# A windowed-attention and gated feed-forward kernel: the same 2127 works issued in another order

## The chip, the cores and the metric

One core of a Trainium2 chip. The metric is the device time of one execution in microseconds (us). Half a per cent of it, 2.6 us, is about the least that a measurement of this kernel can tell from nothing. The engines are PE (matrix products), DVE, ACT and POOL (elementwise work), and SP, which here only issues transfers. Each has its own queue and works through it strictly in order.

## The reference

Attention over 8 batches, 8 heads, 576 tokens and 64 dimensions per head, where each token sees itself and the 63 before it; its output, as rows of 512 numbers, goes through a gated feed-forward block with a convolution over three tokens:

```python
scores = scale * np.matmul(q, k.transpose(0, 1, 3, 2))
mask = (rel >= 0) & (rel < window)
scores = np.where(mask, scores, -1000000000.0)
scores = scores - np.max(scores, axis=-1, keepdims=True)
attn = np.exp(scores)
attn = attn / (np.sum(attn, axis=-1, keepdims=True) + 1e-09)
x = np.matmul(attn, v)
...
h = np.maximum(x @ w_in, 0.0)          # 512 -> 1024
for k in range(K):                     # K = 3 taps over the tokens
    conv_out += conv_w[k][None, None, :] * hp[:, k:k + S, :]
gate = 1.0 / (1.0 + np.exp(-conv_out))
return (h * gate @ w_out)              # 1024 -> 512
```

All inputs to the products are 32-bit; the three weights arrive as 64-bit words and are decoded on the chip.

## The kernel before, in words

The 4608 tokens are cut into 12 units of 384 tokens (six blocks of 64). For each unit the attention makes x, four chunks c of 128 features by 384 tokens; then eight blocks f of 128 hidden features follow, worked in pairs.

One unit, as a chain of works: `load_*` (SP) bring queries, keys and values. `scores` (PE) fill banks of PSUM. `row_max` (DVE) adds a mask and takes the row's maximum, so it waits for scores and mask. `exps` (ACT) takes exponentials with their sums; `guard` (DVE or POOL) adds 1e-9, `reciprocal` (DVE), `normalise` (DVE or POOL). In units 0 and 1 (64-row blocks) PE turns the result (`turn`, `unturn` copies it out); later units use DVE's `transpose` and `place` transfers. `values` (PE) multiplies by v into a bank, and `split_hi` (a rounded copy, xh) and `split_lo` (the rest, xl, always DVE) write x as two parts.

Then per block f: `mm1` (PE, 12 matmuls: each of four chunks with w_hi.xh, w_lo.xh, w_hi.xl), `relu` (ACT or DVE, empties the bank into `hbuf`), `conv_mid` and two `conv_side` (the three taps), and per pair `sigmoid` (ACT), `gate` (DVE or POOL), `gate_hi` and `gate_lo` (the two parts gh, gl), and `mm2` (PE, three matmuls each). `result` copies the sums out and `store` writes them. Units 0 to 2 do f 0 to 3 first, in turn, and f 4 to 7 later (`TASKS`), since the weights are still arriving and being decoded.

Decoding a weight block: `load_w` (SP), `magnitude` (ACT or DVE), `shift`, `sign` (DVE), `low` (ACT), `add_low` (DVE), `larger` (any of three: the rounded part) and `lo` (DVE or POOL: the rest). Two buffers `wx` pass from one block to the next.

Three masks are made by POOL (`make_mask`): mask 0 for units 0 and 1 (`first_masks`), mask 1 for all other blocks and mask 2 for blocks at a sequence's start (`later_masks`; the first such 32-row block comes in unit 3). `fill` issues matmuls on a spare tile, whose results nobody uses.

The order of all this is no scheduler's: `plan()` numbers the 2127 works, and the table `ORDER` lists these numbers in the order of issue. A letter behind a number (A, D, P) sets the engine (ACT, DVE, POOL) of a work that has a choice; `/k` sets its PSUM bank; `Fn/k` is n fill matmuls into bank k. Works on one engine keep the table's order; between engines semaphores on the data and on the buffers decide.

Of the kernel before, what the change touches and what calls it, by code (L numbers as in the profile page):

```python
# [120 lines left out]
def plan():  # L121
# [121 lines left out]
    41 7 13 3 80 9 5 6 86 4 8 0 81 F5/0 40/2 97 1 59/4 42 22/6 43 60 198 31/2 82 83 23 32 195 44 194 24 87D F3/0  # L243
    12/4 45D 46 88 25 89 50/6 33 14 193 26P 47P 196 34 27 197 51 28P F2/1 48/0 11 15 10 35D 16 36 29/1 37D 139
    84 98D 62 38/4 17D 18 99 61 19P 30D 220/2 39D 52 63P 95 20/5 85 211 64 53 221 65P 210/6 21A 54D 49A 55 F1/1
    201/2 212 56P 101 229/4 66/1 222 202 154 57/0 506 67A 100 248/6 58A 238/2 102 90 74/1 249 214 103P 315 138
    104P 77/0 230 213 118 71/7 75A 91 239 231 68/6 215P 78D 92P 204 216 76 93P 72D 69A 79 141A 217P 70 203 73
    316 223 F5/4 94/1 117 140D 142 199 251 224D 225 148 232 226P 240 218/4 144 143 120A 227/5 205P 105/0 242 145
    228D 317 146P 250 440 206 2 207D 168 96A 119A 233D 147D 208/6 241 321/2 234 121 209A 122 153/7 219A 127 107A
    252P 323 243P 235P 123 106D 149 318 260/1 253 124 326 200 257/0 254P 244 322 261A 155A 262 319 327 245P 258D  # L250
    324 150 343 F3/6 246/5 110A 108 236/6 325 109 255/4 111 332/2 247A 328P 256A 125D 151P 329 237A 333 637 152P
    128 439 334 169 335 F3/1 263/7 112 336 357/2 330P 259 338 264D 266/1 265 337 359 126P 156/0 113 320 331 638
    339P 340 341D 267A 114P 342 157A 161A 268 350 363 358 F3/5 269/7 353 368 129 354 158D 351 170D 130A 356 346
    272/0 270 361 162 347 131D 360 345 163 349 362 159 643/2 639 160 115A 352 290/1 364D 365 366D 171A 355 271A
    344 116P 367 174 348 164 645 293/7 369 371 172 173 376 274A 175 133/5 370 165D 378 134/6 176A 273A 379 132/4
    178 166A 640 136 291 377 179 177D 135 277A 373 275 137 442A 167D 374 384/0 292A 380 276 294A 375 381/1 295A
    644 445 372 183 278 441A 279 184 385A 443 654/2 280 180 185 382A 386 801 181P 649 655 390/7 182P 383 387/0
    656 455 188 281P 298A 642 388D 391A 641 186 389 660 469 392 678/2 521 659 449 490 187 470 299 282A 491 393/1
    300 802 191A 283D 450 647 296 657 396/0 444 297 658 679 301 661P 446 286/6 451 414/7 447P 680 394 662 302P
    189D 395A 190A 417/1 475 192 398A 452D 471A 415 663D 397A 285/5 303A 399 288 496 304D 284/4 418A 401A 289  # L260
    400 416A 287 402 472A 403 305 448D 308 404 453D 306 803 419A 493D 520 307 405D 492A 646 310 420 454/0 494
    495 501 497 500 309 498A 473 422A 457/1 499D 311A 313A 502 648 406D 505/7 407D 684 456A 650P 423 480 503D
    681 408/4 504D 474 683 410/6 476 508/0 312A 479 458A 314 682 651 421 804 481 459A 409/5 462A 424 413 509A
    460 425 545/1 461 685D 677 652D 531 411 426P 686 653 507A 412 664 548/0 668 463 427A 464 672 477A 428D 666
# [36 lines left out]
    1464 1236 1467 1483D 1123 1127A 1268/7 1251D 1126D 1255A 1504 1256 1220/4 1237 1257 1622 1357/0 1128 1465
    1462 1360/1 1497 1222/6 1358A 1238P 1361A 1221/5 1469 1362 1223 1359 1225 1505P 1391 1506 1254 1271/1 1239A
# [542 lines left out]
```

## Time and profile before

| | |
|---|---|
| median of three runs | 519.61 us (517.9 to 519.64) |
| profiled execution | 519.21 us, of it the span 517.4 us |
| mean granted clock of PE | 0.997 |
| PE busy | 503.0 us, 97% of the span |
| DVE, ACT, POOL busy | 399.6, 335.4, 167.2 us |

A time in a row of the profile counts from the start of the span. A timeline row has start, duration, engine, line, operation, output and inputs, count, and in brackets how long the engine had been idle before and what ended that. A row of the groups has the busy sum, the mean duration in ns, and the idle time before. Lines are those of the kernel before.

### The profile page before, as it was taken

What the parts mean: (1) busy time and instruction counts of PE and PEld (TensorE: products, weight loads), DVE (VectorE), ACT (ScalarE), POOL (GpSimd) and SP (SyncE); (2) the same over time, 40 slices, a digit from 0 to 9 for tenths busy, and PEclk for the clock granted to TensorE, in tenths of its full rate; (3) what the DMA queues carried; (4) which work ended last, traced back from release to release, by engine and by line L of the source; (5) the groups of instructions that cost most, each with busy time, mean ns of one, the idle gap of its engine ahead of it and who ended that gap; (6) DMA issues with size and microseconds to landing.
All of it is one profiled execution on the core that took longest, in us unless ns stands there. A gap on an engine that the chain in (4) does not pass through costs nothing.

```text
span 517.4 us, 13998 instructions
## 1 busy us (share of the span) xinstructions
PE 503.0 (97%) x5377; PEld 441.3 (85%) x5377; DVE 399.6 (77%) x1197; ACT 335.4 (65%) x922; POOL 167.2 (32%) x261
## 2 busy tenths in 40 slices
PE   8888979999999999999999999999999999999997
PEld 5677859988898898888888899889889889989996
DVE  5989989898968697887687768778585657675881
ACT  5999788986875865883782784792388386332420
POOL 5678233033340400340332241061335332212311
PEclk9999989999999999999999999999999999999999
DMA  8987339332544452364554165355234411400022
GB/s 300 359 352 245 114 110 346 148 112 70 194 101 141 85 186 78 101 165 126 179 181 139 29 197 169 110 177 174 58 106 154 150 64 63 148 6 2 1 99 84
DMA packets 27714, 72.76 MB, mean 141 GB/s; under 512 B 5760, under 2 KB 14080, under 8 KB 27648
## 3 DMA queue, kind: packets, MB, share of 16 engines
q1 hardware_dynamic: 27216, 69.52, 40.8%
q0 software_dynamic: 432, 2.36, 2.6%
q8 instruction: 42, 0.69, 0.5%
q14 instruction: 24, 0.20, 0.1%
HBM read 48.26 MB, written 11.80 MB: 116 GB/s over the span
## 4 chain that ended last, share of the span: by engine, by line
PE 86%; DVE 10%; POOL 2%; issue 1%; ACT 1%; POOLq 0%; DVEq 0%
PE bank L718 36%; PE bank L639 36%; PE bank L622 6%; PE bank L536 5%; PE bank L723 3%; DVE s L557 3%; DVE c L688 1%; DVE wx L453 1%; POOL mask L491 1%; DVE xl L632 1%; DVE s L583 1%; DVE T L602 1%; DVE wx L446 1%; DVE sm L572 1%; POOL mask L493 0%
## 5 line engine op out<-in xcount | busy, mean ns | idle before, releaser
L639 PE MATMUL bank<-xh,w_in 128*128 128x384 f32 x768 | 196.6, 336 | 0.3 <-DVE xl L632 0.2
L718 PE MATMUL bank<-w_out,gh 128*128 128x512 f32 x528 | 169.6, 402 | 0.0
L639 PEld LDWEIGHTS bank<-xh,w_in 128*128 128x128 f32 x768 | 139.4, 188 | 7.1 <-ACT hbuf L665 0.4
L639 PE MATMUL bank<-xl,w_in 128*128 128x384 f32 x384 | 129.1, 336 | 0.7 <-DVE xl L632 0.7
L688 DVE SCALAR_TENSOR_TENSOR c<-hbuf,cw,c 128x386 f32<-128x386 f32 (+1 forms) x192 | 122.8, 661 | 8.8 <-ACT c L681 7.3
L718 PEld LDWEIGHTS bank<-w_out,gh 128*128 128x128 f32 x528 | 96.1, 188 | 19.4 <-issue 0.3
L567 ACT ACTIVATE s<-s,nm 128x96 f32<-128x96 f32 (+2 forms) x288 | 105.2, 368 | 9.2 <-DVE nm L557 8.9
L718 PE MATMUL bank<-w_out,gl 128*128 128x512 f32 x264 | 104.6, 396 | 0.0
L699 POOL TENSOR_TENSOR c<-c,hbuf 128x386 f32<-128x386 f32 (+5 forms) x44 | 50.8, 1171 | 145.2 <-ACT c L692 145.2
L665 ACT ACTIVATE hbuf<-bank 128x384 f32<-128x384 f32 x70 | 33.4, 486 | 67.0 <-PE bank L639 64.9
L639 PEld LDWEIGHTS bank<-xl,w_in 128*128 128x128 f32 x384 | 72.1, 188 | 1.1 <-DVE xl L632 1.0
L557 DVE CUSTOM_DVE_ANT_0 s<-bank,mask 128x96 f32<-128x96 f32 (+2 forms) x288 | 56.4, 254 | 18.2 <-PE bank L536 12.2
L692 ACT ACTIVATE c<-c 128x772 f32<-128x772 f32 (+1 forms) x48 | 40.7, 849 | 30.7 <-DVE c L688 30.4
L718 PEld LDWEIGHTS bank<-w_out,gl 128*128 128x128 f32 x264 | 49.7, 188 | 11.8
L567 ACT ACTIVATION_READ_ACCUMULATOR s<-s,nm 128x1 f32 x288 | 54.4, 189 | 0.0
L583 POOL TENSOR_TENSOR s<-s,r 128x768 f32<-128x768 f32 (+1 forms) x24 | 33.9, 1414 | 49.3 <-DVE r L576 49.1
L681 ACT ACTIVATE c<-hbuf,cw 128x386 f32<-128x386 f32 (+1 forms) x59 | 35.6, 613 | 17.5 <-DVE hbuf L667 8.9
L622 PEld LDWEIGHTS bank<-ub,v 128*64 128x64 f32 x1152 | 35.7, 138 | 9.4 <-issue 3.6
L536 PEld LDWEIGHTS bank<-qk 64*32 64x32 f32 (+1 forms) x2112 | 30.7, 113 | 14.0 <-issue 7.2
L622 PE MATMUL bank<-ub,v 128*64 128x64 f32 x1152 | 38.7, 224 | 3.2 <-ACT hbuf L665 2.8
L536 PE MATMUL bank<-qk 64*32 64x96 f32 (+2 forms) x2112 | 40.5, 260 | 1.3 <-DMA qk<-in_first_dram 0.7
L709 DVE TENSOR_TENSOR gl<-c,gh 128x768 fp32r<-128x768 f32 (+1 forms) x33 | 32.8, 995 | 6.4 <-ACT gh L704 6.0
(79 smaller groups left out, 538.1 us busy)
## 6 DMA issues: line engine op xcount, KB each, us to landing
v<-in_v_dram SPq DMA_DIRECT2D x24, 768.0 KB, 5.6
ub<-T SPq DMA_DIRECT2D x240, 48.0 KB, 2.0
qk<-in_k_dram SPq DMA_DIRECT2D x20, 448.0 KB, 5.0
out_dram<-ot SPq DMA_DIRECT2D x11, 768.0 KB, 4.5
qk<-in_q_dram SPq DMA_DIRECT2D x20, 384.0 KB, 4.2
raw_in<-in_w_in_dram SPq DMA_DIRECT2D x8, 512.0 KB, 8.3
raw_out<-in_w_out_dram SPq DMA_DIRECT2D x8, 512.0 KB, 8.8
qk<-in_first_dram SPq DMA_DIRECT2D x12, 320.0 KB, 4.9
```

The source lines that it names most:

```text
L536: nc.tensor.matmul(banks[bank[h]][r:r + rows, i * P + o:i * P + k], qq[hs, s:s + rows], kk[hs, s + o:s + k], start=True, stop=True)
L557: nc.vector.tensor_tensor_reduce(out=ss[n // NB][:, n % NB, h, o:k], in0=banks[bank[h]][:, i * P + o:i * P + k], in1=mask[m][:, o:k], scal ...
L567: nc.scalar.activation(x, x, AF.Exp, bias=small(nms, (n,))[:, h:h + 1], scale=-1.0, accum_out=small(sms, (n,))[:, h:h + 1])
L583: engine[on].tensor_tensor(sv, sv, small(rs, ns).unsqueeze(2).broadcast_to([P, 2 * len(ns), k]), ALU.mult)
L622: nc.tensor.matmul(banks[bank[0]][h * D:(h + 1) * D, t * W:(t + 1) * W], vs[:, c, t, h], ub[g][:, 2 * p:2 * p + 2, 2 * t + h], start=True, ...
L639: nc.tensor.matmul(banks[bank[0]][:, :NX], w[:, a, c], y[x][:, c], start=(c == 0 and j == 0), stop=(c == NC - 1 and j == 2))
L665: nc.scalar.activation(out, ps, AF.Relu)
L681: nc.scalar.activation(c, h, AF.Copy, scale=w)
L688: nc.vector.scalar_tensor_tensor(c, h, w, c, op0=ALU.mult, op1=ALU.add)
L692: nc.scalar.activation(both(u, j), both(u, j), AF.Sigmoid)
L699: engine[on].tensor_tensor(c[:, :, a:a + n], c[:, :, a + o:a + o + n], h[:, :, 1 + a + o:1 + a + o + n], ALU.mult)
L718: nc.tensor.matmul(banks[bank[0]], x, wts["out", f][:, w], start=(start and i == 0), stop=(stop and i == 2))
```

## The change

Only the table `ORDER` is another; every one of its 100 lines differs, so a line of it tells nothing. The same 2127 works are issued; the fill matmuls are 22 where they were 25.

```
-    41 7 13 3 80 9 5 6 86 4 8 0 81 F5/0 40/2 97 1 59/4 42 22/6 43 60 198 31/2 82 83 23 32 195 44 194 24 87D F3/0
...
```

Engines, of the works that have a choice (before, after): gate 27 on POOL and 21 on DVE, now 21 and 27; relu 70 on ACT and 26 on DVE, now 63 and 33; conv_mid 59 on ACT and 37 on DVE, now 55 and 41; split_hi 24 and 24, now 29 on ACT and 19 on DVE; normalise 24 on POOL and 18 on DVE, now 22 and 20; magnitude 11 on ACT and 5 on DVE, now 9 and 7; larger 6 on ACT, 4 on DVE, 6 on POOL, now 8, 2, 6; lo 6 on POOL and 10 on DVE, now 9 and 7; gate_lo keeps 33 on DVE and 15 on POOL, but not the same ones. `gate_lo` of the very first pair goes from POOL to DVE.

POOL at the program's start, before. Names end in a serial number; mask0, mask1 and mask2 are the three masks, s0 to s2 the score tiles, ident the identity for the turns.

```order
L493 AFFINE_SELECT mask2_77<-mask2_77 32x96
L496 MEMSET mask2_77 32x32
L487 MEMSET mask0_75 128x128
L491 AFFINE_SELECT mask0_75<-mask0_75 64x128
L493 AFFINE_SELECT mask0_75<-mask0_75 64x128
```

After, from the first instruction of the kernel's own on:

```order
L549 MEMSET s0_81 128x2x64
masks.py:197 MEMSET ident_78 128x128
masks.py:199 ISA
masks.py:199 AFFINE_SELECT ident_78<-ident_78 128x128
L648 MEMSET hbuf_69 128x2x2
L649 MEMSET hbuf_69 128x2
L654 MEMSET hbuf_69 128x2
L549 MEMSET s1_82 128x2x64
```

Eight rows of mask 2's selects stood ahead of mask 0 and now come much later; ahead of mask 0 there are now the identity, the blanks and memsets of `hbuf`. Mask 1 follows right behind mask 0, and mask 2 is made here, in the middle of the normalisations of units 0 and 1:

```order
L473 TENSOR_TENSOR w_in0_474<-wx0_70,w_in0_474 128x512
L583 TENSOR_TENSOR s0_81<-s0_81,r0_90 128x512 x2
L487 MEMSET mask2_77 128x128
L491 AFFINE_SELECT mask2_77<-mask2_77 32x96
L493 AFFINE_SELECT mask2_77<-mask2_77 32x96
L496 MEMSET mask2_77 32x64
```

So POOL carries mask 2 at a time when DVE has decoding and splitting to do.

SP at the program's start, before. raw_in0 and raw_in1 are the first two blocks of w_in, cbits the convolution's weights, and `first` the packed queries and keys of units 0 and 1, burst by burst.

```order
L407 DMA qk_79<-in_first_dram 128x640
L428 DMA cbits_74<-in_conv_w_dram 128x48
L407 DMA qk_79<-in_first_dram 128x640 x3
L424 DMA raw_in0_151<-in_w_in_dram 128x1024
L407 DMA qk_79<-in_first_dram 128x640 x2
L424 DMA raw_in1_182<-in_w_in_dram 128x1024
L407 DMA qk_79<-in_first_dram 128x640 x6
```

After:

```order
L407 DMA qk_79<-in_first_dram 128x640
L424 DMA raw_in1_121<-in_w_in_dram 128x1024
L407 DMA qk_79<-in_first_dram 128x640 x5
L424 DMA raw_in0_176<-in_w_in_dram 128x1024
L407 DMA qk_79<-in_first_dram 128x640 x6
```

The block raw_in1 comes right behind the first burst, ahead of the other eleven; raw_in0 stands behind six bursts where it stood behind four; the convolution's weights come later.

ACT around the relus of unit 1 in its first turn, before. w_out2 is the rounded part of a weight block, raw_* the words that `low` works on.

```order
L692 ACTIVATE c1_94<-c1_94 128x772
L681 ACTIVATE c0_93<-hbuf_69,cw_73 128x386
L469 CAST w_out2_1071<-wx0_70 128x512
L665 ACTIVATE hbuf_69<-bank0_104 128x2x192
L704 CAST gh1_96<-c1_94 128x2x384
L449 ACTIVATE raw_out3_812<-raw_out3_812 128x512
L681 ACTIVATE c0_93<-hbuf_69,cw_73 128x386
L436 ACTIVATE wx1_71<-raw_in5_586 128x512
L665 ACTIVATE hbuf_69<-bank1_105 128x2x192
```

After:

```order
L692 ACTIVATE c1_94<-c1_94 128x772
L449 ACTIVATE raw_out3_711<-raw_out3_711 128x512
L665 ACTIVATE hbuf_69<-bank0_104 128x2x192
L449 ACTIVATE raw_in4_930<-raw_in4_930 128x512
L449 ACTIVATE raw_out2_720<-raw_out2_720 128x512
L704 CAST gh1_96<-c1_94 128x2x384
L665 ACTIVATE hbuf_69<-bank1_105 128x2x192
L469 CAST w_out2_1084<-wx0_70 128x512
```

The cast of w_out2, which stood ahead of the relus, stands behind them.

More of the change, by code (lines that the diff above doesn't have):

```diff
@@ L248 @@
[L248 to L252, printed above, removed]
@@ new lines @@
+    96A 227/4 85 251 143 317 218/5 145 199 246/7 106A 107A 208/6 252D 146D 147D 151A 321/2 120A 119D 153/0 152P
+    209A 322 110A 253 123 121 232 108 156/1 127 228A 318 155A 233P 219D 200 254P 128 169 234 323 325 168 235P
+    260/0 157D 326 129 255/6 327 122 236/4 256A 109 261A 124 324 F2/5 332/2 111 247A 125P 257/1 237A 328P 333
+    637 130P 161A 491 263/7 131P 334 258A 319 336 329 264D 343 338 265 330D F3/5 266/7 337 357/2 112 335 162
+    267A 259 339P 126P 113 262 638 340 268 320 341P 359 F3/5 269/1 439 171A 331 170A 114P 342 363 358 272/0 350
@@ new lines @@
+    506 508/1 684 677 668 479 683 666 459D 672 460 507A 685P 409/5 674 474 509A 513A 676 412 461 435A 476 670
+    818/2 480 686 514 667 545/7 477A 687D 675 510A 671 437A 478P 688 465 314 820 430 699 548/0 481 669 515 673
+    526 466D 482A 694 690 819 566/1 546 698 547A 511 467A 689 512 483D 693 516 569/7 468D 642 522A 696 523D 821
+    524 665 842/2 517D 691 433 700 525 695 567 843 486/6 714 436A 697 527 484/4 568A 692 550D 485/5 528A 549D
+    518A 487 844 553A 488 551 848 529D 489 519D 822 701/1 570A 554 710/0 574A 530 707/7 846 552 535 711A 532
@@ new lines @@
+    702A 555 536 823 533P 703 807/2 556 575 534P 591/1 808 965 824 557D 537 809 592 540 593D 845 538 571D 558D
+    847 539 712 559P 594/1 543A 541D 966 542A 813 825D 572 704/0 826 595A 827P 812 560/4 805 705A 438 562/6 810
+    706 561/5 576 599A 612/1 573 708A 811 849D 600 601 577 850 709 615/0 851D 841 578P 852 564 713/7 862 613
+    579A 735 859 616A 854 580D 614A 565 857 596D 583 597 856 814D 716/0 861 598 815 967 816D 602 864 620A 817
+    582 617A 828 563 603D 835 581 832 584 621 863 618 586 839 619 734/1 589A 622 840 587A 855 604A 968 715A 585
@@ new lines @@
+    1131 753 869A 1015P 766 870 751 754 781D 731 991D 749 767P 867 779/0 1132 978D 590 979 980D 970 877/7 780A
+    782 768A 1005 784A 981 880/1 769D 783 771 785 881A 752 786 879A 992 774 787 1016 898/0 788P 1023 1027 1146/2
+    1024 900D 941 789A 1018 885D 901/1 1022 790D 1019 886 1025 1148 792 995 902A 1147 770 903A 996 906A 772 994
+    904 1152 773 882D 999 887 1021 791 907 997 1170/2 908 1028 905 775 969 883 909 998 793 1171 1017 796 884
+    1002 919/7 1172 1020 888 910D 1026 1175 1000 889P 795 993 922/0 1003 920 890D 921A 1004 911D 940/1 1176 1001
@@ new lines @@
+    891P 923A 1149 794 942A 1063 1135/2 1173 1042 912P 1150 1038/7 1293 799A 1032/0 1039D 1174 636 1035/1 1040
+    797A 924D 1029/7 798A 1136 1151 892/4 1033D 1030A 1137 894/6 1153P 1177P 1036A 927A 895 1031 1139 1178 1294
+    897 928 1138 1154 893/5 929 925 915 1141 1034 918 1140 926 896 1179D 930 943/7 1142P 1037 945A 914 931D 944A
+    1041/0 1295 1155D 932A 1169 948A 933P 1180 917 1044/1 1143 1181 949 1191 1144P 1192 935 1296 1045A 1183 913
+    1049A 946 1190 1062/7 1084 1145 947 950 916 1050 951 938 1156 1043A 1051 936 1157 1064A 1046D 1310/2 1134
@@ new lines @@
+    1047 1185 1048 1065/1 1184 1311 1182 952D 1186 1083/0 1158 953D 1166 954D 1133 1312 1067A 956 1066D 1316
+    1334/2 1189 1070D 1068 1161 959 1071 1165 1335 939 1315 1160 957 1336 1187 1085A 934 1052 1188 1069 937 1072
+    1299/2 1073 955 1053D 1457 1314 1162 1086/7 1074D 1164 1075D 1168 1054D 1167 1340 1202/1 1301 1055P 1159
+    1199/0 962D 1203A 1087A 960 1204 1313 1200D 1458 958 963A 1300 1163 1317P 1104/7 1091A 800 1318 1319D 1304
+    1298 1338 1201 1076D 1058/6 1339 1057/5 1337 1061 1088A 1459 1341P 1193/1 1105 1303 1206 1106D 1196/0 1092
@@ new lines @@
+    1194A 1305 1060 961D 1197A 1093 1079 1302 1198 1078 1195 1082 1089 1107/7 1109D 1306D 1110 1307 1333 1308P
+    1056/4 1460 1108D 1205/0 1111 1112A 1090 1309 1094 1208/1 1342 1113 1343D 1095P 1344 1059 1209A 1226/7 1346
+    1297 1114 1347 1227 1320 1115 1348 1081 1096D 1327 1207D 1474/2 1097P 1353 1229/1 1321 1476 1326 1475 1116P
+    1479 1352 1100 1247/0 1325 1210D 1248 1322 1211 1351 1117D 1230D 1349 1498/2 1249A 1118D 1350 1213A 1077
+    1477 1332 1214 1250/1 1356 1478 1212 1345 1499 1330 1215 1080 1331 1228D 1216 1355 1103 1234D 1235 1354 1121
@@ new lines @@
+    1251D 1329 1099 1500 1480 1323 1102 1236 1124 1217D 1098 1502 1120 1370 1503 1123 1363/0 1501 1126D 1366/7
+    1218A 1231D 1232 1101 1504 1233 1463/2 1364A 1367D 1505P 1481P 1237 1269 1482 1219P 1268/1 1368 1621 1465
+    1328 1324 1252A 1119 1270D 1127A 1221/5 1255D 1365 1271/7 1238D 1256 1239A 1622 1464 1122 964 1272A 1253
+    1222/6 1125A 1257 1360/1 1254 1357/0 1483D 1361A 1258 1220/4 1506 1362 1358A 1223 1259P 1469 1623 1359 1225
+    1461 1369/7 1240P 1468 1467 1372/1 1507P 1273A 1466 1624 1243 1276A 1470D 1471 1260D 1371A 1224 1472P 1497
@@ new lines @@
+    1241 1508 1244 1274 1242 1517 1391 1373D 1128 1245 1473 1390/0 1484 1261D 1489 1487 1638/2 1277 1377A 1513
+    1278 1374A 1246 1496 1275 1264 1639 1512 1279 1267 1515 1640 1262 1518 1375 1491 1662/2 1644 1490 1393/7
+    1663 1493 1494 1280D 1642 1509 1664 1263 1488 1433 1412 1495 1265 1281D 1667 1378 1511 1627/2 1668 1379 1519
+    1411/1 1641 1282D 1486 1516 1643 1394D 1785 1398D 1520 1645P 1392D 1283 1376 1485 1266 1646 1395D 1514 1380
+    1285 1396 1492 1399 1284 1462 1628 1286 1510 1400 1414/7 1381P 1629 1786 1288 1415A 1397 1287 1382A 1413D
@@ new lines @@
+    1432/0 1401 1383D 1632 1402P 1530/7 1524/1 1434A 1531D 1534 1291A 1555 1527/0 1532 1647P 1631 1289D 1521/7
+    1626 1528A 1787 1386/6 1290A 1403D 1522A 1389 1404D 1630 1385/5 1665 1523 1384/4 1529 1525A 1388 1419D 1633
+    1661 1435/7 1416A 1420 1437A 1526 1666 1417 1533/0 1669D 1436D 1670 1671D 1440A 1788 1625 1418 1292 1407
+    1438 1387 1421 1406 1441 1422 1409 1442 1634D 1405 1635 1672 1636P 1536/1 1423D 1410 1424D 1554/7 1576 1637
+    1648 1439 1660 1802/2 1425D 1556A 1682 1443 1408 1679 1803 1537A 1655 1557/7 1541A 1444D 1659 1805 1656
@@ new lines @@
+    1445D 1649 1804 1426 1658 1558D 1428 1680 1446D 1826/2 1653 1575/1 1654 1828 1675 1535D 1650 1832 1538D 1652
+    1559D 1806 1431 1539 1657 1808 1429 1827 1684 1427 1562D 1673 1829 1542 1447 1677 1540 1807 1578/7 1676 1543
+    1678 1809P 1560 1544 1651 1561 1683 1449 1810 1563 1681 1430 1564 1579A 1674 1450 1545D 1565 1452 1546D 1830
+    1791/2 1698 1577D 1547P 1688/0 1793 1949 1455A 1691/7 1792 1797 1566P 1694/1 1689D 1453A 1692D 1448 1794
+    1550/6 1795 1811D 1451 1567A 1597 1693 1553 1695D 1831 1950 1596/7 1583D 1584 1796 1696 1580A 1798P 1833D
@@ new lines @@
+    1585 1685/1 1690 1825 1548/4 1834 1799 1686D 1551 1800P 1454D 1599/0 1687 1456 1568D 1789 1951 1581 1549/5
+    1600A 1835D 1552 1598A 1601A 1569 1801 1570 1582 1571 1602 1586 1697/1 1812 1836 1843 1604A 1700/0 1587D
+    1790 1844 1588A 1740 1719 1573 1589D 1701A 1574 1603 1952 1718/7 1817 1705D 1605 1841 1706 1823 1606 1818
+    1591 1607 1822 1594 1848 1699A 1721/0 1702A 1821 1720A 1847 1703 1704 1838 1966/2 1707 1820 1722D 1592 1816
+    1708 1967 1837 1739/1 1968 1839 1970 1846 1608D 1842 1572 1845 1609A 1590 1819 1741A 1990/2 1610P 1824 1971
@@ new lines @@
+    1814 1742/7 1992 1840 1815 1709D 1726A 1813 1969 1595 1723D 1991 1996 1760/0 1724 1994 1710D 1993 1727
+    1955/2 1728 1995 1725 1593 1743A 1997P 1761 1729 1613 1762D 1612 1711D 1858/1 1747D 1972 1748 1849/7 1730D
+    1855/0 1616 1749 1954 1859A 1973P 1957 1611 1856D 1615 1961 1860 1614 1619A 1956 1852/1 1960 1744D 1857
+    1714/6 1617A 1974 1618A 1745 1717 1853A 1731D 1958 1713/5 1850D 1732P 1716 1998 1959 1851 1763/0 1854 1746
+    1975P 1861/7 1764A 1750 1999P 1989 1864/1 1765A 1862 1883 1768A 1962P 1751P 1963 2000 1734 1882/0 2006 1964D
@@ new lines @@
+    1752A 2002 2012 1904 1766 1735 1620 1965 2003 1738 2011 1712/4 1863D 2001 1769 1715 2009 1865D 1733 1753D
+    1953 1736 1770 1737 1866D 1756 1976 1767 1759 1988 1885/7 1771 1984 1985 1884A 1772D 2005 2010 1903/1 1773D
+    2007 1774D 1986 1886D 1983 1869D 1755 1887D 1981 1870 1754 1982 1867 1906/0 1978 1868 1987 1871 2008 1888
+    1872 1757 1979 1890A 1777 2004 1873P 1977 1758 1980 1780 1925 1776 1874A 1779 1905A 1875P 2022/7 1782A 1907A
+    2019/1 2023D 1783A 2016/0 2024 1891 2013/7 2017A 1911D 1775 2020D 1892 1778 1889 1878/6 2021 1781A 1877/5
@@ new lines @@
+    2018 1893 1784 1881 1908A 1894P 1876/4 1924/1 1895A 1927/0 1896D 2014D 1912 1880 2015 1928A 1909 1899 1926A
+    1932A 1929D 1898 1930 1902 1913 2025/7 1910 1933 1914 1931 1915D 2028/0 1916D 1934 1917P 1879 1935 2048/1
+    2026 2049 2027D 2029A 1936P 1901 2033A 1897 1919 2030D 1920 2072 1937D 1923 2095 2031 1900 2032 2051/0 1938D
+    2050D 2034 1941 2052A 1944 2056D 2035 1922 2057 1918 2036 2071/7 2053A 2037P 2074/1 2054 2038A 2058 2055
+    2073D 1921 2039D 1940 2075D 1943 2076D 2079A 1939 2059 2094/0 2080 1947A 2060D 2077 2061A 2043/7 2081 1942
@@ L343 @@
+    1946A 2078 2097/1 2062D 2082 2083P 2041/5 2098D 2045 2096D 2102A 2042/6 2099D 2047 1945D 2046 2084D 1948
+    2040/4 2085D 2044 2064 2100 2068 2103 2087 2101 2066 2104 2063 2091 2105 2067 2065 2106P 2086 2069 2090
+    2107D 2070 2108D 2089 2093 2088 2109 2112 2092 2116 2113 2125 2123 2110 2117D 2114 2118 2111 2119D 2124 2115
+    2126 2120 2121A 2122
 """
```

115 lines of the change are left out of this document (21 added, 94 removed).

## The prediction

> **What bounds the kernel now.** I read the page's busy shares first, then the waits of PE, then windows over the front, then the timelines of DVE, ACT and POOL at the places where PE waits.
>
> ```profile
> span 517.4 us, 13998 instructions
> PE 503.0 (97%) x5377; PEld 441.3 (85%) x5377; DVE 399.6 (77%) x1197; ACT 335.4 (65%) x922; POOL 167.2 (32%) x261
> ```
>
> PE is the bound: of 517.4 us it is idle for only 14.4. Where PE waits, in full (us in total, times, longest):
>
> ```profile
> PE bank L590 <- POOL s L583: 3.2, 4, 1.1
> PE bank L622 <- ACT hbuf L665: 2.8, 2, 1.9
> PE bank L402 <- DVE spare L755: 1.5, 1, 1.5
> PE bank L639 <- DVE xl L632: 1.0, 2, 0.7
> PE bank L536 <- DMA qk<-in_first_dram: 0.7, 2, 0.6
> PE bank L622 <- DVE hbuf L667: 0.5, 1, 0.5
> PE bank L536 <- issue: 0.5, 1, 0.5
> PE bank L590 <- DVE s L583: 0.4, 1, 0.4
> ```
>
> They sum to 10.6 us; the 3.8 us missing from 14.4 lie behind the last matmul (513.37 + 0.33 = 513.7, against 517.4), where one result is copied and stored. When the waits come, and at what clock, the windows show (start and end; busy us of PE, weight loads, DVE, ACT, POOL; granted clock; DMA share; GB/s):
>
> ```profile
> 5.00:10.00 5.00, 4.47 (x51) 3.06 (x51) 3.72 (x35) 3.10 (x17) 1.53 (x6) 1.00 0.99 361
> 65.00:70.00 5.00, 2.25 (x42) 1.59 (x43) 5.00 (x11) 4.29 (x9) 0.95 (x2) 1.00 0.53 145
> 70.00:75.00 5.00, 5.00 (x91) 3.52 (x87) 3.79 (x16) 4.97 (x11) 1.92 (x5) 0.66 0.21 41
> 75.00:80.00 5.00, 5.00 (x123) 3.92 (x122) 4.51 (x19) 4.47 (x16) 1.87 (x5) 1.00 0.66 211
> 80.00:110.00 30.00, 30.00 (x158) 27.83 (x157) 28.33 (x63) 26.63 (x70) 5.99 (x10) 1.00 0.62 233
> 110.00:140.00 30.00, 30.00 (x405) 25.95 (x404) 28.06 (x77) 22.95 (x63) 11.95 (x15) 1.00 0.39 122
> 513.37 0.33 PE L723 MATMUL bank<-gl,w_out 128*128 128x386 f32 x1
> ```
>
> From 70 us on PE is full. So whatever the new order does after that can only lose time; all gain must come out of the front: 9.1 us of waits (without the first 1.5, which stays), the slow clock at 70 to 75 us (0.34 x 5.00 = 1.7 us), and matmuls that are only fill.
>
> **The change part by part.** No work is added or removed except fills (25 before, 22 now). What counts is which work stands ahead of which, and on which engine. DVE is 90% busy or more from 65 us to 140 us but for 70 to 75, so in the front DVE's lateness becomes PE's.
>
> First, DVE's two waits for masks, and the place where it stood blocked:
>
> ```profile
> 3.88 0.92 PE L536 MATMUL bank<-qk 64*64 64x64 f32 x16
> 6.25 0.22 DVE L557 CUSTOM_DVE_ANT_0 s<-bank,mask 128x64 f32<-128x64 f32 x1 [4.85 <-POOL mask L493]
> 37.18 0.26 DVE L557 CUSTOM_DVE_ANT_0 s<-bank,mask 128x96 f32<-128x96 f32 x1 [1.13 <-POOL mask L493]
> 58.50 2.05 POOL L709 TENSOR_TENSOR gl<-c,gh 128x768 fp32r<-128x768 f32 x1 [5.06 <-ACT gh L704]
> 58.77 1.81 DVE L572 TENSOR_SCALAR sm<-sm 128x8 f32<-128x8 f32 x1
> ```
>
> Before, POOL makes mask 2, for blocks at the start of a sequence and first needed in unit 3, ahead of mask 0, which the first row maximum needs. Now mask 0 is made first, behind an identity and a few small memsets only. I take it that it no longer decides: the scores are there at 3.88 + 0.92 = 4.80, and DVE can begin at about 4.9 instead of 6.25, a gain of 1.35. The price is in SP's queue: 512 KB of w_in1 now stand ahead of the remaining pieces of `first`, at 361 GB/s (window 5 to 10 us) 1.4 us later for those; the decode of w_in1, which DVE now does early, can fill that. I take the full 1.35; the other end is 0. The second mask wait (1.13) goes because mask 1, for which DVE waited there, is now made right behind mask 0. The third is a guard of 128x8 that took 1.81 beside POOL's gate_lo, where its group takes 0.32 on the mean (next fence): 1.5 lost. That gate_lo is now DVE's own work. Together 1.35 + 1.13 + 1.5 = 4.0 us off DVE.
>
> A page bears on the third. The Trainium skill, "SBUF — State Buffer", section "SBUF: two separate sides", says that GpSimd and VectorE share one port pair that one instruction holds to its end while the other engine blocks; this row agrees, the guard ending as POOL's operation ends. By that rule mask 2, which moves into DVE's full stretch, would give back some of these gains; that case is priced below from rows.
>
> Against this, DVE gets more to do. Ahead of the last split of unit 2 (`split_lo` of x chunk 3) DVE now has in addition 2 gate_lo, 2 add_low, 2 sign, 2 guard, 1 gate_hi, 1 unturn, and not 2 split_hi, 1 gate, 1 magnitude.
>
> ```profile
> L709 DVE TENSOR_TENSOR gl<-c,gh 128x768 fp32r<-128x768 f32 (+1 forms) x33 | 32.8, 995 | 6.4 <-ACT gh L704 6.0
> L453 DVE CUSTOM_DVE_ANT_0 wx<-raw_out,wx 128x1024 uint16<-128x1024 uint16 x8 | 5.8, 722 | 0.2
> L446 DVE SCALAR_TENSOR_TENSOR wx<-raw_out,wx 128x512 uint32<-128x512 uint32 x8 | 5.4, 694 | 0.1
> L572 DVE TENSOR_SCALAR sm<-sm 128x8 f32<-128x8 f32 (+1 forms) x20 | 6.5, 324 | 2.2 <-ACT s L567 2.0
> L627 DVE CAST xh<-bank 128x384 fp32r<-128x384 f32 x24 | 13.2, 550 | 10.1 <-PE bank L622 10.0
> L699 DVE TENSOR_TENSOR c<-c,hbuf 128x2 f32<-128x2 f32 (+5 forms) x36 | 22.0, 647 | 4.2 <-ACT c L692 3.9
> ```
>
> I set the gate_hi against one split_hi (both copies of a block) and the unturn against the magnitude. The rest: 2 x 0.995 + 2 x 0.722 + 2 x 0.694 + 2 x 0.324 = 5.5; less 0.550 and one gate, 22.0 / 21 gates = 1.05: 3.9. Neighbours overlap by some 0.1 us (as on ACT below: 65.71 + 0.62 against 66.24), so five more instructions net are about 3.4. DVE's balance at unit 2's x is then 3.4 - 4.0 = **-0.6 us**.
>
> Further on, ahead of unit 3's first split, the surplus is 3 gate_lo, 2 gate, 2 conv_mid, 2 magnitude, 3 guard, 1 row_max pair, 1 gate_hi, 1 unturn, less 2 split_hi, 2 larger and 1 lo: by the same kind of sum, an estimate, 5.6 us, so DVE would be 1.6 us later there than before. In the windows 75 to 140 us DVE has 0.49 + 1.67 + 1.94 = 4.1 us idle, which covers 1.6. I cost it at nothing; the point at which that cover is gone is a rival below.
>
> Second, the relus of unit 1 on ACT, which hold the banks that PE needs for unit 2's values:
>
> ```profile
> 65.71 0.62 ACT L469 CAST w_out<-wx 128x512 fp32r<-128x512 f32 x1 [3.12 <-DVE wx L453]
> 66.24 0.48 ACT L665 ACTIVATE hbuf<-bank 128x384 f32<-128x384 f32 x1
> 66.77 0.92 PE L622 MATMUL bank<-ub,v 128*64 128x64 f32 x24 [0.85 <-ACT hbuf L665]
> 66.70 0.84 ACT L704 CAST gh<-c 128x768 fp32r<-128x768 f32 x1
> 67.44 0.66 ACT L449 ACTIVATE raw_out<-raw_out 128x512 uint32<-128x512 uint32 x1
> 69.07 0.84 ACT L665 ACTIVATE hbuf<-bank 128x384 f32<-128x384 f32 x2
> 69.59 0.92 PE L622 MATMUL bank<-ub,v 128*64 128x64 f32 x24 [1.90 <-ACT hbuf L665]
> ```
>
> ACT stood 3.12 us before a weight cast that waited for DVE, with the relu queued behind it. In the new order the cast stands behind both relus. The first wait (0.85) goes. Between the two relus there were gate_hi, low, conv_mid and magnitude, 69.07 - 66.70 = 2.4 us; now there are two lows and a gate_hi, 0.74 + 2 x 0.57 with the overlap taken off, about 1.8, so the second wait shrinks by 0.6. Sum for ACT: **-1.45 us**. It adds to DVE's -0.6, because the values wait for a bank, and what DVE brings, the splits, comes after them.
>
> Fills stand where PE waits anyway; three fewer cost or bring nothing by themselves. The moves of SP's loads behind 20 us I cost at nothing: no wait of PE or DVE in the lists above names a weight load. The tail: the last pair's gate moves from DVE to POOL and its gate_lo the other way.
>
> ```profile
> L699 POOL TENSOR_TENSOR c<-c,hbuf 128x772 f32<-128x772 f32 x2 | 4.1, 2058 | 10.0 <-ACT c L692 10.0
> L709 POOL TENSOR_TENSOR gl<-c,gh 128x772 fp32r<-128x772 f32 x1 | 1.9, 1876 | 8.3 <-DVE gh L704 8.3
> 489.84 0.96 DVE L699 TENSOR_TENSOR c<-c,hbuf 128x772 f32<-128x772 f32 x1
> ```
>
> The gate costs 2.06 - 0.96 = 1.1 more, gate_lo 1.88 - 0.995 = 0.9 less: 0.2 on a path behind which PE still has a queue of mm2 from the pair before. Nothing, unless that queue runs dry; the last copy and store stay.
>
> **Sum.** -0.6 - 1.45 = -2.05. The profiled execution took 519.21 (1.8 around its span), so 517.2; the median of the three runs, 519.61, lies 0.4 above it, so **517.6 us**. The slow-clock stretch I leave as it is.
>
> On that stretch the Trainium skill, "TensorE: Matmul & The Clock Gate", section "What's actually happening", says that the clock halves after an idle window of about 3.4 us and that these windows run free of the program. Here it was 0.66 over 70 to 75 us though PE's longest wait was 1.90; PE was busy 2.25 of 5 us before. Whether it returns is open.
>
> **The rivals.** Faster by half a per cent (2.6 us) is about what can be told from no change here.
>
> A, the front wins more: the slow clock goes (1.7) with the waits as forecast, 519.6 - 2.05 - 1.7 = 515.9; at the far end both waits on ACT go altogether (2.75): 519.6 - 0.6 - 2.75 - 1.7 = 514.6. For it: that stretch has 2.75 of 5 us idle just ahead of the slow clock, and a shorter wait may keep the clock. Against it: something must replace ACT as the last to arrive, and DVE is full there (5.00 of 5.00).
>
> B, gained and given back: mask 2 is now made by POOL under DVE's work and holds DVE up.
>
> ```profile
> 1.29 0.26 POOL L491 TENSOR_SCALAR_AFFINE_SELECT mask<-mask 32x96 f32<-32x96 f32 x1
> 32.74 0.63 POOL L491 TENSOR_SCALAR_AFFINE_SELECT mask<-mask 32x96 f32<-32x96 f32 x1
> ```
>
> It is eight selects; in the quiet start POOL took 0.26 for each, so at worst 8 x 0.26 = 2.1 us are lost to DVE, and -2.05 becomes 0: 519.6. Against it: while mask 1 was made from 32 us on, under DVE's work, it was POOL that was slowed, to 0.63 a select. The rule of the shared port quoted above allows either.
>
> C, slower: DVE cannot carry its extra work. It is 1.6 us late at unit 3's first split, with 4.1 us of idle time to take it from. Each further meeting with a POOL operation costs what the guard lost, 1.5 us. One is still covered (3.1); from the second on PE waits before mm1 of unit 2 or 3. Five give 1.6 + 7.5 - 4.1 = 5.0, and 517.6 + 5.0 = 522.6. For it: nothing in PE's queue hides a late x. Against it: POOL has fewer, not more, of the long operations in the front.
>
> **How the numbers follow.** The forecast, with DVE's first gain between 0 and 1.35 and ACT's between 0.85 and 2, lies at 517.0 to 519.5; chance 0.42. A 0.31, all of it under 517.0, B 0.17, C 0.10. Faster (under 517.0): A, 0.31; slower (over 522.2): C, 0.10, whose lower part is made up by late waits not named; the same 0.59. The range leaves out C and the far end of A: 515.0 to 520.2.
>
> **What would show it.** First row maximum at about 4.9 us and no wait of DVE for a mask; the wait of the values on ACT's relu at or under 1.3 us in all; the window 65 to 70 with PE over 3 busy; no wait of PE behind 75 us. A wait before mm1 for xl (L632) behind 80 us would show C; row maxima and casts on DVE stretched while POOL makes the second mask would show B; a clock of 1.00 throughout from 15 us on, A. A wait for gl or gh in front of L723 near 505 us would show the tail's sum wrong.

## The result, and the profile after

| | before | after |
|---|---|---|
| median | 519.61 us (517.9 to 519.85) | 516.06 us (515.93 to 516.24) |
| ratio | | 0.9939 (95% interval 0.9923 to 0.9954) |
| profiled execution, its span | 519.21, 517.4 us | 516.15, 514.3 us |

The new order is 3.5 us faster. The forecast was 517.6 with a range of 515.0 to 520.2: inside the range, but at the place of rival A (515.9), not of the likeliest case.

The page after, its busy shares:

```profile
span 514.3 us, 13994 instructions
PE 500.2 (97%) x5374; PEld 437.9 (85%) x5374; DVE 405.0 (79%) x1211; ACT 330.7 (64%) x916; POOL 152.2 (30%) x253
```

PE is idle for 514.3 - 500.2 = 14.1 us, against 14.4 before. So nearly all of the 3.1 us of span came out of PE's busy time, although PE has the same products to compute. The totals hide an exchange. In the first 30 us PE is busy for 23.6 us where it was for 25.3 (three fills fewer, and scores of unit 0 that took 0.67 us for 16 products at 6.49 us, where they had taken 1.13 at 5.37), but it waits longer there, so this is no gain. Between 65 and 75 us it waits 2.4 us less, and the stretch at half clock is gone. The windows after (start and end; busy us of PE, weight loads, DVE, ACT, POOL; granted clock; DMA share; GB/s):

```profile
60.00:65.00 5.00, 4.02 (x21) 3.34 (x19) 4.97 (x21) 2.38 (x5) 1.16 (x3) 1.00 0.32 71
65.00:70.00 5.00, 4.68 (x121) 3.61 (x120) 4.89 (x9) 4.54 (x9) 0.00 (x0) 1.00 0.39 121
70.00:75.00 5.00, 5.00 (x123) 3.69 (x121) 4.99 (x22) 4.97 (x14) 1.93 (x2) 1.00 0.56 186
75.00:80.00 5.00, 5.00 (x36) 4.36 (x32) 5.00 (x11) 5.00 (x23) 2.27 (x4) 1.00 0.96 347
110.00:140.00 30.00, 30.00 (x348) 26.25 (x347) 26.14 (x91) 26.99 (x77) 9.17 (x13) 1.00 0.42 121
```

The stretch from 65 to 70 us, where PE was busy for 2.25 of 5 us, is now at 4.68, and no slow clock follows it: 70 to 75 us is at 1.00 where it was at 0.66. PE's waits after, the six longest of fourteen lines (us in total, times, longest):

```profile
PE bank L402 <- DVE spare L755: 1.5, 1, 1.5
PE bank L536 <- DMA qk<-in_first_dram: 1.3, 3, 0.6
PE bank L639 <- POOL w_in L473: 1.1, 1, 1.1
PE bank L590 <- POOL s L583: 1.0, 2, 0.8
PE bank L718 <- ACT w_out L469: 1.0, 1, 1.0
PE bank L718 <- DVE gl L709: 0.8, 1, 0.8
```

The waits for relus (2.8) are gone and those for normalisations fell from 3.2 to 1.0. In their place stand waits for parts of weights (1.1 and 1.0), for gl (0.8) and 0.6 more for the first loads.

The clock differs between executions of the same program. Medians here leave out the few runs that were disturbed and took hundreds of microseconds longer. Over all experiments 90 runs of the kernel before remain, with their mean granted clock: 24 at 0.999 or 1.000, median 518.05 us; 24 at 0.996 to 0.998, which is one stretch of 3.4 us at half clock, 519.6; 33 at 0.990 to 0.995, two or three such stretches, 520.0; 8 at 0.987 to 0.989, 522.3; and a single one at 0.949 that took 517.99 all the same, which stays open. The new kernel's five runs stood at 1.000 four times and once at 0.998. So of its 3.5 us about 519.6 - 518.05 = 1.55 is the clock and 518.05 - 516.1 = 1.95 the order itself at full clock; this is an estimate from the groups of runs.

### The profile page after: what moved, and what is told of

Its sections match the earlier page's. It is cut to its first block, busy times and chain, and to the rows that moved or that the text cites. A ratio compares the mean times of both kernels' runs of the same rounds, so it can differ in the third digit from the quotient of the medians.

```text
span 514.3 us, 13994 instructions
## 1 busy us (share of the span) xinstructions
PE 500.2 (97%) x5374; PEld 437.9 (85%) x5374; DVE 405.0 (79%) x1211; ACT 330.7 (64%) x916; POOL 152.2 (30%) x253
## 4 chain that ended last, share of the span: by engine, by line
PE 88%; DVE 9%; POOL 1%; issue 0%; ACT 0%; DVEq 0%
PE bank L639 37%; PE bank L718 36%; PE bank L622 6%; PE bank L536 5%; PE bank L723 3%; DVE s L557 2%; DVE c L688 1%; DVE s L583 1%; DVE wx L442 1%; DVE wx L446 1%; DVE T L602 1%; PE bank L402 0%; DVE wx L453 0%; DVE xl L632 0%; DVE ub L595 0%
## 5 line engine op out<-in xcount | busy, mean ns | idle before, releaser
L699 POOL TENSOR_TENSOR c<-c,hbuf 128x386 f32<-128x386 f32 (+5 forms) x36 | 39.1, 1103 | 110.2 <-ACT c L692 110.2
L665 ACT ACTIVATE hbuf<-bank 128x384 f32<-128x384 f32 x63 | 30.0, 485 | 62.4 <-PE bank L639 60.9
L709 POOL TENSOR_TENSOR gl<-c,gh 128x768 fp32r<-128x768 f32 x15 | 28.2, 1879 | 72.9 <-DVE gh L704 36.5
L681 ACT ACTIVATE c<-hbuf,cw 128x386 f32<-128x386 f32 (+1 forms) x55 | 33.2, 614 | 25.6 <-DVE hbuf L667 11.6
L536 PEld LDWEIGHTS bank<-qk 64*32 64x32 f32 (+1 forms) x2112 | 28.9, 108 | 14.1 <-issue 6.9
L536 PE MATMUL bank<-qk 64*32 64x96 f32 (+2 forms) x2112 | 38.1, 251 | 1.6 <-DMA qk<-in_first_dram 1.3
L709 DVE TENSOR_TENSOR gl<-c,gh 128x768 fp32r<-128x768 f32 (+1 forms) x33 | 31.4, 952 | 10.4 <-ACT gh L704 10.0
```

The costliest lines, as they stand in the source:

```text
L536: nc.tensor.matmul(banks[bank[h]][r:r + rows, i * P + o:i * P + k], qq[hs, s:s + rows], kk[hs, s + o:s + k], start=True, stop=True)
L665: nc.scalar.activation(out, ps, AF.Relu)
L681: nc.scalar.activation(c, h, AF.Copy, scale=w)
L699: engine[on].tensor_tensor(c[:, :, a:a + n], c[:, :, a + o:a + o + n], h[:, :, 1 + a + o:1 + a + o + n], ALU.mult)
L709: engine[on].tensor_tensor(gls[j % 3][:, :, :n], cs[j % 2][:, :, :n], ghs[j % 3][:, :, :n].bitcast(F32), ALU.subtract)
```

## The experiments

Theory: the gain is made in the front, by PE's waits between 40 and 70 us and the slow clock that follows them; after that PE is full and the order can only lose. The rival puts part of it into the rest or the tail. Each kernel was run beside the kernel before, whose medians were 519.27, 519.65, 519.27 and 519.75 us in the four groups.

To see where a lead is made, the table gives the work that PE has begun by a time, each product at its mean start-to-start duration from the rows, fills left out, less the same of the kernel before. It is worked out from the traces of the profiled executions, so it holds their slow stretches too: new_rest, which has the old order until 95 us, is behind at 75 and 90 us because its trace has 6.8 us at half clock from 69 us on, where before has 3.4. In us:

| at | after | new_front | cut69 | masks_late | gate_ahead | new_rest |
|---|---|---|---|---|---|---|
| 30 | 0.5 | 0.5 | 0.5 | 0.0 | 0.0 | 0.0 |
| 45 | 2.5 | 2.5 | 2.5 | 0.7 | -0.1 | 0.0 |
| 65 | 1.0 | 1.0 | 1.0 | 0.8 | -0.1 | 0.0 |
| 75 | 4.4 | 4.4 | 2.3 | 0.5 | 2.1 | -0.7 |
| 90 | 4.7 | 4.8 | 2.6 | 0.7 | 2.0 | -1.3 |
| 300 | 3.6 | 4.6 | 2.5 | 0.6 | 2.0 | -2.5 |
| 500 | 3.6 | 4.6 | 2.5 | 0.6 | 2.0 | -2.8 |

**new_front and new_rest: front and rest exchanged.** The two orders have done nearly the same works after 468 entries of the table (PE at 89 us after, at 95 us before), so each front can go with the other rest.

```
new_front: the new table's first 468 entries, then the old table without the works in them
new_rest:  the old table's first 468 entries, then the new table without the works in them
```

> The new order up to its mm2 at about 89 us, then the remaining works in the old order (the two orders have 13 works apart there). Theory F, all of the gain is made before 85 us: in PE work done, the new order is 4.7 us ahead there, and 1.1 of it is lost later in the new order's own rest, so the old rest should keep most of it: 515.0 to 515.9, median at or under the new kernel's 516.1. Rival: the later order and the tail matter too, then above 517.

> The old order up to about 94 us of PE, then the remaining works in the new order. Theory F: 519.6 to 520.7 (no gain, and the 1.1 us that the new rest loses). Rival, part of the gain lies in the rest or the tail: 518.5 or less.

new_front took 514.43 us, ratio 0.9906 (0.9886 to 0.9926): faster than both kernels, and no later run is clearly faster. new_rest took 521.82 us, ratio 1.0048 (1.0028 to 1.0069). All of the gain is in the first 89 us, and the new rest costs 1.6 to 1.7 us, with the new front as with the old (516.06 - 514.43 = 1.6; at full clock 519.7 - 518.05 = 1.65). No wait explains that loss: PE has none behind 95 us in the traces of either, of before or of after. By the table the new kernel loses 1.1 of its lead between 90 and 300 us, and it is PE's own sequence. Start to start, an mm2 takes 0.70 us among its like, 0.79 when a block of scores or values follows and 0.80 when one came before; an mm1 takes 2.08, and 2.19 next to scores. The works that both orders have behind 100 us (some 408 us), priced by their neighbours in this way, sum to 1.1 us more in the new sequence, which breaks runs of products more often (mm1 right behind scores 11 times, not 3). In the new kernel's trace another 0.5 us lie behind the last matmul:

```profile
510.18 0.48 ACT L731 COPY ot<-bank 128x386 f32<-128x386 f32 x1 [1.94 <-PE bank L723]
```

From the start of this last copy to the end of the span it is 4.1 us after, 3.7 before (513.74 to 517.4). The last data land at 512.8, 2.6 us behind the copy's start, and the program ends 1.5 us later, where before it ended 1.1 after its last landing. But this is not the new rest's: new_rest ends with the same works in the same order (its line numbers are 5 lower), and from its last copy to the end of its span of 520.1 it is 3.6 us.

```profile
516.54 0.48 ACT L726 COPY ot<-bank 128x386 f32<-128x386 f32 x1 [1.94 <-PE bank L718]
```

Why the new kernel's end took longer is open. So the sequence is shown for 1.1 of the 1.6 to 1.7 us; in new_rest's trace the works from 90 us on lose 1.5.

**new_start, cut47, cut69: where in the front.** The same exchange with earlier cuts, at PE's 31, 47 and 69 us.

> The new order up to about 31 us of PE, then the old order. In PE work done the new order is only 0.5 us ahead at 30 us. If that lead is all that the start gives: 519.1. If what counts is that DVE is earlier (first row maximum at 4.9, masks 1 and 2 made by then), the waits at 65 to 70 us and the slow clock shrink too: 516 to 517.5.

> The new order up to about 47 us of PE, then the old one. It tells where the front's gain is made. PE's work done is 2 us ahead at 45 to 55 us. If a lead carries over: 517.5. If the old order's waits at 65 to 70 us do not depend on what came before, since DVE is the one that sets them and has the same queue: 518.5 to 519.5, with slow stretches as before.

> The new order up to about 69 us of PE (behind unit 2's first two values), then the old one. If what counts is the stretch from 47 to 69 us, it is as fast as the new front to 89 us: 514.4 to 515. If the order of 69 to 89 us matters too: 516 or more.

new_start 518.89 us, ratio 0.9991 (0.9975 to 1.0007): the start alone gives about 0.4, which can't be told from nothing. cut69 516.64, 0.9938 (0.9915 to 0.996): most of it, and by the table it has the new front's lead until 70 us. Then it loses 2.1 us in one wait:

```profile
72.34 1.94 PE L622 MATMUL bank<-ub,v 128*64 128x64 f32 x48 [2.11 <-POOL c L699]
```

The gate named in brackets, which ends at 72.15, can hardly be the cause: these values read nothing of it, and the relu that frees the first one's bank ends at 70.5. They do read `ub`, and the last two transfers of `place` into it land at 72.0 and 72.6. The old order asks for these values right behind the first two, while new_front does two mm2, scores and a third mm2 first, and begins them at 73.69 without a wait. So the loss belongs to this join of front and rest; that it hangs on the transfers is read from the trace, not tried. The expectation "as fast as new_front" failed by 2.2. cut47, 519.17 (0.999, 0.9975 to 1.0005), says nothing: its join leaves a split of x so late that PE waits 5.94 us for xl at 54 us.

**masks_only and masks_late: the prediction's first two terms.** The old order, but POOL makes mask 0 and mask 1 at the start; mask 2 goes to where mask 1 stood (32 us), or to 53 us.

```
- 41 7 13 3 80 9 ... 0 81 F5/0 40/2 97 1 59/4 ... 440 206 2 207D ... 268 ... 270 361
+ 41 7 13 80 9 ... 0 81 F5/0 40/2 97 1 2 59/4 ... 440 206 3 207D ...            (masks_only)
+ 41 7 13 80 9 ... 0 81 F5/0 40/2 97 1 2 59/4 ... 440 206 207D ... 270 3 361    (masks_late)
```

> The old order with one move: POOL makes mask 0, identity, mask 1 at the start and mask 2 where mask 1 stood. DVE's two waits for masks (1.35 of the first, 1.13) should go. If DVE's lateness becomes PE's, as the prediction has it: 519.6 - 2.5 = 517.1. If other waits take their place (the next scores wait for their loads, ACT's relus stay behind the cast): 519 to 520, no change.

> As masks_only, but mask 2 is made at 53 us, where POOL stood idle, and not at 32 us, where it held up POOL's normalisations (PE's wait for one was 3.0 there). DVE's two waits for masks go and nothing is queued behind the mask. If the prediction's first two terms (1.35 + 1.13 on DVE) reach PE: 519.4 - 2.5 = 516.9, and 515.6 among runs at full clock (before: 518.1). If DVE's lead is used up by waits for loads and ACT before 60 us, as the flat first 30 us of the other runs suggest: 518.5 to 519.5, or no change at full clock.

masks_only was if anything slower, 520.71 us, ratio 1.0021 (1.0001 to 1.0041). DVE did start at 4.97, but mask 2 has memsets that mask 1 lacks and ends at 38.1 and not 37.1, three normalisations of unit 1 queue behind it on POOL, and PE waits for one of them (this kernel's table has fewer lines, so its line numbers are 4 lower):

```profile
42.62 1.53 PE L586 MATMUL bank<-ident,s 128*128 128x128 f32 x12 [2.95 <-POOL s L579]
...
40.00:50.00 10.00, 7.38 (x192) 5.91 (x193) 8.94 (x29) 7.85 (x29) 9.53 (x11) 0.83 0.58 203
```

The wait was 1.06 before; now a stretch of half clock follows it too. masks_late, with nothing queued behind the mask, took 518.46, ratio 0.9972 (0.9961 to 0.9984): 1.3 us gained where the two DVE waits are worth 2.5. By the table the lead is 0 at 30 us and 0.7 at 90. So about half of what DVE wins there reaches PE (by the interval 0.8 to 2.0), and only if POOL's queue is clear.

**glo_on_dve: the third term.**

```
- 344 116P 367
+ 344 116D 367
```

> The old order, the very first gate_lo on DVE and not on POOL. By the prediction's third term DVE's guard beside it no longer takes 1.81 (1.5 less), against 0.9 of its own: DVE is 0.6 earlier, and with it the gate that PE's wait at 69 us hangs on: 519.6 - 0.6 = 519.0, slow stretches as before. If POOL's next long operation meets DVE instead: no change or up to 1 us more.

518.2 us, ratio 0.9975 (0.9956 to 0.9994), 1.1 us gained where 0.6 was expected. The guard beside which POOL's gate_lo had run took 0.17 and not 1.81:

```profile
60.60 0.17 DVE L572 TENSOR_SCALAR sm<-sm 128x8 f32<-128x8 f32 x1
```

The mechanism holds. But in the new order POOL puts another operation there, a gate, and DVE's normalise loses as much beside it:

```profile
58.40 1.85 POOL L699 TENSOR_TENSOR c<-c,hbuf 128x2 f32<-128x2 f32 x2 [3.31 <-ACT c L692]
58.64 2.43 DVE L583 TENSOR_TENSOR s<-s,r 128x768 f32<-128x768 f32 x1
```

2.43 against 0.96 in the old order: 1.47 lost, the same 1.5 again. The normalise ends 0.8 us behind the gate (61.07 against 60.25), so it was held for most of the gate. The Trainium skill, "SBUF — State Buffer", section "SBUF: two separate sides", says that a DVE operation with two SBUF inputs and a GpSimd (POOL) operation that reads SBUF contend for one port pair, and that the second to start blocks until the first ends; these two rows agree.

**cast_behind and gate_ahead: the ACT term.** In the old order the cast of w_out2 goes behind the relu of unit 1's f 2; then DVE's gate of unit 0's second pair also goes ahead of the decoding.

```
- 164 645 ... 134/6 176A 273A ... 370 165D 378 ... 179 177D 135 ... 292A 380
+ 164 645 ... 134/6 273A ... 370 165D 378 ... 179 135 ... 292A 176A 177D 380    (cast_behind)
+ 164 165D 645 ... 134/6 273A ... 370 378 ... 179 135 ... 292A 176A 177D 380    (gate_ahead)
```

> The old order with one move: the cast of w_out2 on ACT (and its lo on DVE) goes behind the relu of unit 1's f 2. By the prediction's ACT term PE's two waits for relus (2.75) shrink by 0.85 or more: 518.7 or less, and less again if the slow clock goes. Rival, from the trace of before read again: the relu of f 2 overwrites what the gate of unit 0's second pair still reads, and that gate runs on DVE only at 65.59, behind the decoding; so the second wait grows by what the first loses, and the time stays at 519.3 to 519.8, the slow stretch included.

> As the run before, and DVE's gate of unit 0's second pair goes ahead of the decoding of w_out2, right behind its sigmoid (62.1 us). By the rival of that run both waits go (2.75), and with PE busy at 65 to 70 us the slow stretch too: 519.4 - 2.75 - 1.75 = 515, all runs at a clock of 0.999 or more. If other waits come in their place (the splits of unit 2 on DVE, which stay where they were): 517 to 518.5. If the slow clock does not come from these waits: its runs still spread over two us.

cast_behind: 520.53 us, ratio 1.0011 (0.999 to 1.0032), no gain. The first wait went, the second grew from 1.90 to 2.80:

```profile
65.74 1.02 DVE L699 TENSOR_TENSOR c<-c,hbuf 128x2 f32<-128x2 f32 x2
66.85 0.83 ACT L704 CAST gh<-c 128x768 fp32r<-128x768 f32 x1 [3.72 <-DVE c L699]
69.21 0.48 ACT L665 ACTIVATE hbuf<-bank 128x384 f32<-128x384 f32 x1
69.74 1.55 PE L622 MATMUL bank<-ub,v 128*64 128x64 f32 x24 [2.80 <-ACT hbuf L665]
```

So the link was not quite the expected one. The relu of f 2 does overwrite what that gate and POOL's `carry` read, but POOL was done with it at 66.94. The relu runs at 69.21 because it stands in ACT's queue behind gate_hi, which waited 3.72 us for the gate, and three more works.

gate_ahead: 517.34 us, ratio 0.9955 (0.9936 to 0.9975). The gate runs three microseconds earlier and PE waits no more for a relu; 1.0 us is given back in a wait for w_out2's lo:

```profile
62.83 0.99 DVE L699 TENSOR_TENSOR c<-c,hbuf 128x2 f32<-128x2 f32 x2
...
PE bank L718 <- DVE w_out L473: 1.0, 1, 1.0
...
65.00:70.00 5.00, 3.96 (x57) 2.93 (x56) 4.93 (x13) 4.02 (x9) 0.00 (x0) 1.00 0.49 129
70.00:75.00 5.00, 4.68 (x120) 3.12 (x119) 4.96 (x27) 4.09 (x10) 1.97 (x6) 1.00 0.49 138
```

With PE busy for 3.96 us of 65 to 70, 7 of its 12 runs were at a clock of 0.999 or more, against 24 of 90 for the kernel before. At full clock it gains 0.6 to 0.9 (517.14 and 517.41 at 1.000 and 0.999, against 518.05), so by these groups the larger part of its 2.3 us is the clock.

**decode_first and no_warm: more out of the new front.** Both start from new_front. The first moves two row maxima on DVE behind the decoding of w_out2, for which PE waits 0.97 there; the second leaves out the three fills at 4.7 us.

```
- 445 644 380 174 293/0 645 291 ... 177D 137    (644 and 645 behind 177D in decode_first)
- F3/0                                          (the second group of fills, no_warm)
```

> The new order to 89 us and then the old one (run new_front, 514.4), with one move: on DVE the first two row maxima of unit 3 (1.5 us at 62 us) go behind the decoding of w_out2 and the gate_lo that stood behind them. PE's waits there (0.97 for the cast of w_out2, 0.32 for its lo) should go: 514.4 - 1.0 = 513.4. Rival: the exponentials and the scores of unit 3 come later and PE waits for them instead: 514.4 or more.

> As new_front, without the three fill matmuls between the first and the second scores (4.7 us). In the new kernel the scores behind them took 0.67 for 16 matmuls where before took 1.13. If these fills are what brings the full clock seven microseconds earlier and PE's lateness there passes on: 515 to 516. If PE's start is hidden behind DVE anyway: 514.4 as new_front, or a little less.

decode_first: 514.28 us, no better than new_front within what can be told (0.9907, 0.9881 to 0.9934, against 0.9906). Its lead was 0.7 us larger at 65 us and was given back at 70:

```profile
64.21 0.50 PE L718 MATMUL bank<-w_out,gh 128*128 128x512 f32 x1 [0.19 <-DVE w_out L473]
70.54 0.50 PE L718 MATMUL bank<-w_out,gh 128*128 128x512 f32 x1 [1.29 <-DVE w_out L473]
```

DVE is busy for 4.9 of each 5 us there; what one work gains another pays. no_warm: 514.35 (0.9896, 0.9866 to 0.9925): those fills are worth nothing. The scores behind them do run slower without them, and PE still reaches the first turn at 11.72 us, as in the new kernel, so a faster start of PE is no part of the gain:

```profile
5.90 5.00 PE L536 MATMUL bank<-qk 64*64 64x128 f32 x80 [1.09 <-DMA qk<-in_first_dram]
11.72 0.63 PE L590 MATMUL bank<-ident,s 128*128 128x128 f32 x4 [0.28 <-DVE sm L572]
```

Two of no_warm's six runs took 512.67, faster than any other and at a slightly lower mean clock; which waits they miss is open, as the profile is of one of the others.

## Why the prediction was right, and where not

**What bounds.** Right: all gain lies in the front. PE has no wait behind 75 us in the new kernel, and new_rest alone gains nothing. Which moves make up the front's lead is shown only in part: of 4.7 us at 90 us, gate_ahead has 2.0 and masks_late 0.7, and whether such parts add was not run.

**DVE's balance, -0.6.** At the place that it spoke of -0.8 was measured: the last split of unit 2 ends at 77.68, and at 78.51 before.

```profile
74.51 0.26 DVE L557 CUSTOM_DVE_ANT_0 s<-bank,mask 128x96 f32<-128x96 f32 x1 [1.17 <-PE bank L536]
76.90 0.56 DVE L627 CAST xh<-bank 128x384 fp32r<-128x384 f32 x1 [0.42 <-PE bank L622]
77.49 1.02 DVE L632 TENSOR_TENSOR xl<-bank,xh 128x384 fp32r<-128x384 f32 x2
...
76.20 1.48 DVE L632 TENSOR_TENSOR xl<-bank,xh 128x384 fp32r<-128x384 f32 x3
```

The first three rows are of before, the last of after. That the numbers agree is in part luck. Before, DVE waited 1.17 us for PE's scores and 0.42 for PE's values just ahead of this split, so PE set its time; after, DVE is busy for 12.88 of the 13 us from 65 to 78 and sets it itself. The sum compared DVE's work alone (and nets six instructions more, not five, which makes it -0.7). Of its terms, the first row maximum starts at 4.98 and no mask is waited for, as said, but the third was won and lost again beside POOL's gate.

**The ACT term, -1.45.** This step failed as the prediction put it. The waits did go, yet the cast's move alone is worth nothing, as cast_behind shows. Behind the cast stood a second thing that the prediction did not see: gate_hi of unit 0's second pair stands ahead of f 2's relu in ACT's queue, and the gate that it needs stood on DVE behind the decoding, from 65.59 to 66.61. While the cast held ACT until 65.71, that did not show. With the cast away ACT waits for the gate itself, 3.72 us. What the trace named as releaser, the relu on ACT, was the last link of a chain that began with DVE's order; the row "ACT, L469, waited 3.12 for DVE" was read as the cause, and it was one of two. In the new order the gate is POOL's at 58.40, gate_hi follows at 60.28, and unit 2's first two values take the banks of f 0 and f 3 (relus at 61.02 and 66.28) and not of f 1 and f 2:

```profile
60.28 0.84 ACT L704 CAST gh<-c 128x768 fp32r<-128x768 f32 x1
61.02 0.49 ACT L665 ACTIVATE hbuf<-bank 128x384 f32<-128x384 f32 x1
```

With the cast moved, the gate's move is worth 3.2 us (520.53 to 517.34, the clock included). The gate's move without the cast's was not run.

**The slow clock, left as it is.** This is why the likeliest time was missed by 1.5 us. The wait that was to shrink was also what let the clock fall: rival A had the price, 1.7, and the runs say 1.55. A wait of 2.75 us that goes here would bring 4.3 if nothing took its place; by the table the new kernel's lead grows by 3.4 between 65 and 75 us.

**The rest and the tail, at nothing.** Mis-sized: +1.6, of which PE's own sequence is 1.1; the other 0.5 lie at the end of the program in the new kernel's trace and are not explained. The front gained correspondingly more than the sum said, 518.05 - 514.4 = 3.65 at full clock against 2.05. The two errors cancel, so that the order's own part, 1.95 at full clock, looks like a hit. That is luck.

**Rivals.** B did not happen: mask 2 was made from 28.85 us on under DVE's work, and it was POOL's selects that stretched, to 0.34 to 0.72, not DVE. Its neighbour did, though: masks_only shows a mask in POOL's queue holding up normalisations, and so PE: 1.9 us less work begun at 50 us, and a slow stretch behind it. C did not happen; DVE's lateness stayed within its idle time.

## What to carry to other kernels

A wait on the engine that bounds can be paid twice where the clock falls behind it: look at what the clock does in the window after a wait before pricing it. Follow a releaser to what released it in its turn, through everything that stands ahead of it in its engine's queue, before saying which instruction to move; a single-move kernel settles that for the price of one run. And when two orders differ everywhere, exchange their halves: here the new front with the old rest was faster than either (514.43 us), and no list of waits would have shown the new rest's loss.

## What the runs showed of the hardware that was not expected

The granted clock falls to 0.50 for 3.4 us although PE was not idle: 2.25 us busy of 5 with no wait over 1.90 was enough, in most executions and not in all, while 3.96 of 5 mostly was not. The Trainium skill, "TensorE: Matmul & The Clock Gate", section "What's actually happening", has the length of the window (about 3.4 us) and that it runs free of the program, which fits the spread between runs; it speaks of an idle window, and here half-busy ones did it.

One such stretch costs 1.55 us on the median (518.05 to 519.6), the second and third 0.4 together. Why these cost so little is not shown, but two traces fit a reason: PE lost time that it would have waited anyway, or that fills took. In masks_only's trace one lies partly on three fills (1.65 us at 45.53; 0.96 before). glo_on_dve's trace has half clock from 15.8 to 22.6 us, is 3.2 us behind the kernel before in work begun at 50 us and only 1.1 behind at 75.

A change between the products of the feed-forward (mm1, mm2) and those of the attention (scores, values) costs PE about 0.1 us on either side (0.70 to 0.79 and 0.80 for an mm2), without any wait in the records; ten such changes more behind 100 us (74, not 64) go with the 1.1 us. Between mm1 and mm2 a change costs nothing (0.70).
